# The fourth pair of token tiles of the last stage takes the path of the first three

## The chip, the cores and the metric

The kernel runs on one core of one Trainium2 chip. The core has a matmul engine (TensorE, PE in the profile, with its weight loads shown as PEld), VectorE (DVE), ScalarE (ACT), GpSimd (POOL) and SyncE (SP), each with its own in-order queue of instructions. DMAs are issued here from SP's queue and from ACT's queue. The metric is the device time of one execution in microseconds.

## The reference

Three pieces follow each other: an attention with 32 memory slots, a gated feed-forward layer without an activation, and a second feed-forward layer.

```python
a = softmax(phi, over the sequence)            # batch 4, heads 8, sequence 576, memory 32
k_m, v_m = a.T @ k, a.T @ v                    # per head, 32 x 64
x = softmax(q @ k_m.T / 8) @ v_m               # joined over heads: 2304 tokens x 512
x = ((x @ w_a) * (x @ w_b)) @ w_out            # 512 -> 1536 -> 512
h = x @ w_in                                   # 512 -> 2048
g = h * (1.0 / (1.0 + np.exp(-1.702 * h)))
out = (g @ w_out2).astype(np.float32)          # 2048 -> 512
```

The weights come as 64-bit floats and are decoded on the chip from their two 32-bit words.

## The kernel before

Every product of full precision is made of three matmul passes: each operand is split into a high and a low part (`hi_lo`, lines 305 to 309: ACT copies the high part, DVE or POOL subtracts it from the source for the low one), and high x high, low x high and high x low are added up in PSUM.

The change lies in the last product, g @ w_out2. Its 2304 tokens are nine pairs of tiles (`i` = 0 to 8, 256 tokens each, `NW`), its contraction of 2048 is 16 chunks of 128, and a quarter of it is `K4` = 4 chunks. g lies in DRAM (`g2d`), written by the stage before. For each pair it is loaded transposed (`gated_part`, line 1197), split into high and low parts (`split_part`, line 1220), and multiplied.

- The first `NF` = 3 pairs go by quarters: `load_gated` loads quarter 0 of pairs 0, 1, 2, then quarter 1 of the three, and so on, each 512 KB into a buffer of `f_s`. `proj2` (line 1322) takes the six tiles in that order too, so six PSUM banks are open at a time: each step is 12 matmuls (line 1335) of one tile and one quarter. The first weights chunks of a quarter are needed first, and the decode of the last chunks runs beside the first quarters.
- Pairs 3 and 4 (up to `NS` = 5) go by halves of the contraction: two loads of 1 MB into buffers of `fw_s`; their matmuls are the same `proj2`, one pair at a time.
- Pairs 5 to 8 use seven products in place of eight (`proj2_seven`, line 1349; matmuls in line 1366). Before pair 5 this needs sums of weight blocks, the T weights: `load_pair` (line 1291) loads chunks back from DRAM (`w2d`) by a DMA on ACT's queue (line 1298), DVE and POOL subtract (line 1309), and `hi_lo` splits. Eight such pairs of chunks pass through two buffers, so a batch is two loads, eight subtractions and eight splits, and the next loads wait for the batch before.

The buffers are pieces of the tile `acc`, which the stages before have left. Six quarter buffers exist, F1 to F3 given early, F4 to F6 by `room_last`; a wide buffer is two of them: F5 with F6, F4 with F1, and F2 with F3. In the program as built, the last quarters of pairs 0, 1 and 2 lie in F3, F4 and F5, no quarter uses F6, and the first half of pair 3 goes to F5 with F6. Splits go to six slots in the tiles `attn0` and `attn1` (`attn_92`, `attn_93` in the order's rows); a slot comes free when PE has multiplied the step before in it.

The order of all instructions is made before the launch, by a planner in the kernel (`Order`, lines 95 to 171): streams ask for an engine with an estimated length, or wait for a mark or a buffer, and the planner emits them in the order in which its own clock says they can start. So an instruction that is planned early waits at the head of its engine's in-order queue if what it needs comes later. The weights' raw loads (line 334, `load`) and the decode (`decode_piece`, lines 404 to 453) are streams of the same planner; line 417 is its first step on ACT, line 427 and 432 later ones on DVE, line 448 the high part of a decoded chunk. Outputs are stored by SP (`store`, line 1411), four DMAs for a tile, after ACT or DVE has copied the PSUM bank (`copy`, lines 293 and 295).

The wide buffers are given (`room_last`) when all splits of the first three pairs are planned (the mark "front"), the third of them once the third quarter of pair `NF` is split.

Of the kernel before, what the change touches and what calls it, by code (L numbers as in the profile page):

```python
# [56 lines left out]
def crowded():  # L57
    measured()
    Lengths.pool, Lengths.both, Lengths.slow = 1.3, 1.75, 1.55


def short():
    Lengths.dve, Lengths.act, Lengths.psum = 68, 94, 52
    Lengths.pool, Lengths.both, Lengths.slow = 1.0, 1.0, 1.0
# [110 lines left out]
def tile_mem_attention_moe_moe2(  # L175
# [18 lines left out]
    NT, DM = out.shape  # L194
    F1 = w_o1.shape[0]
    F2 = w_o2.shape[0]
    P = 128
# [19 lines left out]
    K4 = F2 // P // 4  # L217
    NB = 2 * P
# [93 lines left out]
    loaded = {}  # L312
# [415 lines left out]
    def give(slots_, views):  # L728
        slots_.free += [[x, now()] for x in views]
# [202 lines left out]
    win_s, hb_s, f_s, fw_s, sb_s, tb_s = Slots(), Slots(), Slots(), Slots(), Slots(), Slots()  # L932
    wo2_t, blocks = {}, []

    def views(m, n, count, o=0):
        return [m[:, o + i * n:o + (i + 1) * n] for i in range(count)]
# [79 lines left out]
    def room_chunks(*flat):  # L1016
        for x in flat:
            od.mark(now(), "room", "o2", len(wo2))
            wo2.append(x.rearrange("p (i f) -> p i f", i=2))
# [4 lines left out]
    def room_last():  # L1024

        short()
        od.handicap[DVE] = W1
        used = wt["o1", NG1 - 1][0]
        room_chunks(*views(g1_m, CN, 3), *views(used, CN, 2), *views(big["eff_b"], CN, 1))
        for x, o, n in (  # L1030
            (big["y0"], 0, 14), (big["y0"], 18 * DM, 3), (eff_m, 0, 4), (attn_m[0], 4 * SN, 1),
            (attn_m[1], 2 * SN, 5), (big["eff_b"], CN, 2), (p2_rest[0], 0, 4),
        ):
            blocks.extend(x.rearrange("p (i f) -> p i f", i=2) for x in views(x, BN, n, o))
        for q in order:
            for j in range(2):
                for u in range(2):
                    yield "mark", "g2", q, j, u
        n = KD * 2 * N2
        give(f_s, views(acc, FN, 1, n + 2 * FN))  # L1040
        give(tb_s, views(acc, 2 * DM, 2))
        for p in range(F2 // P // 2):
            od.spawn(PT, load_pair(p))
        for c, x in enumerate(views(acc, FN, 2, n), len(pieces) - 3):
            yield "mark", "raw", c
            give(f_s, [x])
        t = yield "mark", "wo2", F2 // P - 1
        crowded()
        od.mark(t, "decoded")
        yield "mark", "front"  # L1050
        wide = views(acc, 2 * FN, 3, n)
        give(fw_s, wide[:2])
        yield "mark", "sb", NF, 2 * K4, 0
        give(fw_s, wide[2:])
        for p in range(F2 // P // 2):
            yield "mark", "wt", p
        short()
        give(dm_s, views(acc, DM, 4))
# [133 lines left out]

    NF, NS, NW = 3, 5, NT // NB

    def gated_part(s, i, o, e):
        t = 0.0
        for g in range(o // G2, (e - 1) // G2 + 1):
            for n in range(i * NB // N2, ((i + 1) * NB - 1) // N2 + 1):  # L1200
                for j in range(2):
                    t = max(t, (yield "mark", "g2", (g, n // 2), j, n % 2))
        f = s[0].rearrange("p (c t) -> p c t", c=e - o)
        nc.sync.dma_start(
            out=f, in_=g2d[o * P:e * P, i * NB:(i + 1) * NB].rearrange("(c p) t -> p c t", p=P)
        )
        od.load(max(t + 2500.0, s[1]), 1.7 * (e - o) * P * NB * 4, "f", i, o)
        loaded["f", i, o] = s, f

    def load_gated():  # L1210
        for o in range(0, 4 * K4, K4):
            for i in range(NF):
                s = yield "slot", f_s
                yield from gated_part(s, i, o, o + K4)
        for i in range(NF, NW):
            for o in (0, 2 * K4):
                s = yield "slot", fw_s
                yield from gated_part(s, i, o, o + 2 * K4)

    def split_part(t, src, *key):  # L1220
        b = yield "slot", sb_s
        loaded[key] = b
        od.spawn(4, split_into(max(t, b[1]), b, src, key))

    def split_into(t, b, src, key):
        t = yield from hi_lo(t, b[0][:, HI], b[0][:, LO], src, K4 * P)
        od.mark(t, *key)

    def split_gated():
        for o in range(0, 4 * K4, K4):  # L1230
            for i in range(NF):
                t = yield "mark", "f", i, o
                slot, f = loaded.pop(("f", i, o))
                for s in range(2):
                    yield from split_part(t, f[:, :, s * P:(s + 1) * P], "sb", i, o, s)
                for s in range(2):
                    t = max(t, (yield "mark", "sb", i, o, s))
                f_s.release(slot, t)
        od.mark(t, "front")
        for i in range(NF, NW):  # L1240
            yield from (split_whole(i) if i < NS else sums_gated(i))

    def split_whole(i):
        for h in (0, 2 * K4):
            t = yield "mark", "f", i, h
            slot, f = loaded.pop(("f", i, h))
            for o in range(0, 2 * K4, K4):
                for s in range(2):
                    yield from split_part(t, f[:, o:o + K4, s * P:(s + 1) * P], "sb", i, h + o, s)
            for o in range(0, 2 * K4, K4):  # L1250
                for s in range(2):
                    t = max(t, (yield "mark", "sb", i, h + o, s))
            fw_s.release(slot, t)
# [9 lines left out]
    def sums_gated(i):  # L1263
        n = K4 * P
        parts = {}
        ts = {}
        for h in (0, 2 * K4):
            ts[h] = yield "mark", "f", i, h
            slot, f = loaded.pop(("f", i, h))
            x = f.rearrange("p (c k) t -> p c k t", k=2)  # L1270
            parts[h] = slot, {
                a: x[:, :, k, s * P:(s + 1) * P]
                for a, k, s in ((A11, 0, 0), (A12, 1, 0), (A21, 0, 1), (A22, 1, 1))
            }
        for name in LAST:
            a = PRODUCTS[name][0]
            for h in (0, 2 * K4):
                t, f = ts[h], parts[h][1]
                if a in MERGE:
                    dst, in0, in1, op, before = MERGE[a]  # L1280
                    for x in before:
                        t = max(t, (yield "mark", "sw", i, h, x))
                    ts[h] = t = yield from combine(t, f[dst], f[in0], f[in1], op, n)
                yield from split_part(t, f[HOME[a]], "sw", i, h, a)
        for h in (0, 2 * K4):
            t = 0.0
            for name in LAST:
                t = max(t, (yield "mark", "sw", i, h, PRODUCTS[name][0]))
            fw_s.release(parts[h][0], t)

    def load_pair(p):

        t = max((yield "mark", "w2d", 2 * p), (yield "mark", "w2d", 2 * p + 1))
        for x in blocks[4 * p:4 * p + 4]:
            wo2_t.setdefault(p, []).append(x)
        m = yield "slot", tb_s
        x = m[0].rearrange("p (k j f) -> p k j f", k=2, j=2)
        nc.scalar.dma_start(
            out=x.rearrange("p k j f -> p k (j f)"),
            in_=w2d[2 * p * P:(2 * p + 2) * P, :].rearrange("(k p) f -> p k f", p=P),  # L1300
        )
        od.load(max(t, m[1]), 2 * P * DM * 4, "pair", p)
        t = max((yield "mark", "pair", p), (yield "mark", "decoded"))
        b11, b12, b21, b22 = (x[:, k, j] for k in range(2) for j in range(2))
        n = DM // 2
        for i, (dst, in0, in1) in enumerate(
            ((b11, b12, b11), (b12, b22, b12), (b22, b22, b11), (b21, b21, b22))
        ):
            t = yield from combine(t, dst, in0, in1, ALU.subtract, n)
            od.spawn(PT, split_t(t, wo2_t[p][i], dst, p, i))  # L1310
        for i in range(4):
            t = max(t, (yield "mark", "wt", p, i))
        tb_s.release(m, t)
        od.mark(t, "wt", p)
# [117 lines left out]
    def main():  # L1432
# [80 lines left out]
        for q in order[1:]:  # L1513
# [3 lines left out]
            if q == (NG2 - 1, 1):  # L1517
                room_split(*views(attn_m[0], SN, 4), *views(attn_m[1], SN, 2))
        od.spawn(9, room_last())
        yield from proj2([(i, s) for i in range(NF) for s in range(2)])  # L1520
        for i in range(NF, NW):
# [66 lines left out]
```

## Time and profile before

| | us |
|---|---|
| median of 3 runs (lowest, highest) | 790.88 (789.92, 791.01) |
| the profiled execution | 790.42 |
| its span on the core | 788.6 |
| PE busy | 772.0 (98%) |
| DVE busy | 638.9 (81%) |
| ACT busy | 417.8 (53%) |
| POOL busy | 365.2 (46%) |

The span is the time from the first to the last instruction of the program on the core; the execution's own time has 1.82 us more. In the page's forty slices PE shows 9 tenths or more in all but the first, the last and one that shows 7, at 651 to 670 us. The last product runs from 584 us to the end.

### The profile page before, as it was taken

How to read it: one execution, taken by the hardware profiler on the slowest of the kernel's cores; microseconds unless marked ns; L12 is line 12 of the kernel's file. 1: busy time of each engine (PE TensorE's matmuls, PEld its weight loads, DVE VectorE, ACT ScalarE, POOL GpSimd, SP SyncE). 2: the span in 40 equal slices, each digit the busy share in tenths (PEclk: the TensorE clock that was granted, in tenths of full speed). 3: DMA queues.
4: the chain of work that ended last, by engine and by line, in shares of the span. 5: the costliest groups of instructions: out<-in, count | busy, mean ns of one | idle time of the engine just before them, and what ended most of it. 6: DMA issues, size and time to landing. Idle time of an engine off the chain costs nothing.

```text
span 788.6 us, 14299 instructions
## 1 busy us (share of the span) xinstructions
PE 772.0 (98%) x5216; PEld 711.6 (90%) x5216; DVE 638.9 (81%) x1135; ACT 417.8 (53%) x925; POOL 365.2 (46%) x343
## 2 busy tenths in 40 slices
PE   8999999999999999999999999999999997999997
PEld 7777789999899899989999999999998885889997
DVE  4888978999999997977989778777867878547886
ACT  4567768564645655445565555555544445434442
POOL 1224225553645644436799655333341046453563
PEclk9999999999999999999999999999999998999999
DMA  8866400122213221230013545455598738624421
GB/s 297 311 190 196 148 25 28 55 81 81 81 54 108 81 81 53 72 90 1 1 65 101 183 159 172 149 164 174 208 309 271 226 135 257 215 75 134 135 81 28
DMA packets 70151, 103.96 MB, mean 132 GB/s; under 512 B 5824, under 2 KB 48832, under 8 KB 70080
## 3 DMA queue, kind: packets, MB, share of 16 engines
q1 hardware_dynamic: 64768, 93.84, 37.3%
q10 hardware_dynamic: 5312, 9.21, 3.3%
q8 instruction: 41, 0.67, 0.4%
q14 instruction: 30, 0.25, 0.1%
HBM read 75.24 MB, written 27.79 MB: 131 GB/s over the span
## 4 chain that ended last, share of the span: by engine, by line
PE 83%; DVE 5%; DMA 4%; ACT 3%; issue 2%; POOL 1%; ACTq 0%; POOLq 0%; DVEq 0%; SPq 0%
PE bank L1135 22%; PE bank L831 18%; PE bank L1366 10%; PE bank L864 10%; PE bank L887 9%; PE bank L1335 6%; PE bank L787 3%; DMA raw<-in_moe_w_out_dram 2%; PE bank L619 1%; PE bank L575 1%; DMA raw<-in_moe_w_b_dram 1%; DVE attn L302 1%; PE bank L756 1%; PE bank L494 1%; DMA acc<-w2d 1%
## 5 line engine op out<-in xcount | busy, mean ns | idle before, releaser
L1177 DVE TENSOR_TENSOR acc<-bank,acc 128x384 f32<-128x384 f32 x168 | 89.7, 553 | 31.8 <-PE bank L1135 20.2
L302 DVE TENSOR_TENSOR attn<-acc,attn 128x512 fp32r<-128x512 f32 (+1 forms) x93 | 88.0, 967 | 30.7 <-ACT attn L308 30.6
L302 POOL TENSOR_TENSOR acc<-acc 128x512 f32<-128x512 f32 (+2 forms) x59 | 76.2, 1306 | 55.7 <-DVE attn L302 30.5
L308 ACT ACTIVATE attn<-acc 128x512 fp32r<-128x512 f32 (+2 forms) x114 | 66.6, 603 | 62.4 <-PE bank L1366 18.7
L1187 ACT ACTIVATE acc<-acc 128x384 f32<-128x384 f32 x96 | 49.3, 523 | 53.1 <-DVE acc L1177 52.2
L844 ACT ACTIVATE gr<-bank 128x288 f32<-128x288 f32 x96 | 38.9, 405 | 64.0 <-PE bank L831 60.9
L302 POOL TENSOR_TENSOR y<-gr,y 128x288 fp32r<-128x288 f32 x40 | 36.3, 908 | 49.9 <-ACT y L308 49.7
L847 DVE TENSOR_TENSOR gr<-bank,gr 128x288 f32<-128x288 f32 x96 | 43.1, 449 | 15.1 <-PE bank L831 8.5
L831 PE MATMUL bank<-attn,eff 128*128 128x288 f32 x384 | 54.4, 296 | 0.0
L831 PEld LDWEIGHTS bank<-attn,eff 128*128 128x128 f32 x384 | 52.1, 188 | 1.3 <-issue 0.9
L864 PE MATMUL bank<-g,whl_b 128*128 128x288 f32 x384 | 52.8, 295 | 0.1
L1135 PE MATMUL bank<-attn,y 128*128 128x384 f32 x288 | 52.3, 335 | 0.0
L864 PEld LDWEIGHTS bank<-g,whl_b 128*128 128x128 f32 x384 | 51.7, 188 | 0.6 <-POOL whl_b L302 0.3
L887 PE MATMUL bank<-y,whl_a 128*128 128x512 f32 (+1 forms) x240 | 51.5, 370 | 0.0
L1335 PE MATMUL bank<-wv,attn 128*128 128x512 f32 x180 | 45.9, 411 | 5.2 <-ACT attn L308 5.2
L1135 PEld LDWEIGHTS bank<-attn,y 128*128 128x128 f32 x288 | 50.1, 188 | 0.0
L419 POOL TENSOR_SCALAR dm<-dm 128x512 f32<-128x512 f32 x21 | 34.7, 1656 | 31.8 <-ACT dm L417 31.7
L887 PEld LDWEIGHTS bank<-y,whl_a 128*128 128x128 f32 x240 | 41.9, 188 | 8.0
L1335 PEld LDWEIGHTS bank<-wv,attn 128*128 128x128 f32 x180 | 35.7, 199 | 13.7 <-ACT attn L308 5.6
L302 POOL TENSOR_TENSOR y<-acc,y 128x256 fp32r<-128x256 f32 (+1 forms) x22 | 19.8, 912 | 59.2 <-ACT y L308 59.2
L302 POOL TENSOR_TENSOR g<-gr,g 128x288 fp32r<-128x288 f32 x28 | 27.0, 966 | 40.8 <-ACT g L308 40.6
L907 DVE TENSOR_TENSOR acc<-bank,acc 128x512 f32<-128x512 f32 (+1 forms) x72 | 38.4, 551 | 5.9 <-PE bank L887 5.2
(269 smaller groups left out, 2022.3 us busy)
## 6 DMA issues: line engine op xcount, KB each, us to landing
g2d<-acc SPq DMA_DIRECT2D x96, 192.0 KB, 2.3
raw<-in_moe_w_out_dram SPq DMA_DIRECT2D x28, 512.0 KB, 4.3
acc<-g2d SPq DMA_DIRECT2D x12, 1024.0 KB, 6.1
raw<-in_moe_w_in_dram SPq DMA_DIRECT2D x16, 512.0 KB, 3.8
acc<-g2d SPq DMA_DIRECT2D x12, 512.0 KB, 5.7
raw<-in_moe_w_a_dram SPq DMA_DIRECT2D x20, 256.0 KB, 2.7
raw<-in_moe_w_b_dram SPq DMA_DIRECT2D x20, 256.0 KB, 3.0
q<-in_q_dram SPq DMA_DIRECT2D x8, 576.0 KB, 6.0
```

What stands on the lines that cost most here:

```text
L302: (nc.gpsimd if e == POOL else nc.vector).tensor_tensor(out=dst, in0=in0, in1=in1, op=op)
L308: nc.scalar.activation(out=hi, in_=src, func=AF.Copy)
L831: nc.tensor.matmul(ps[0][:, :U], e[c][:, sw, i * CW + j * P:i * CW + (j + 1) * P], attn(b, mv, c, u * U, U), start=(n == 0), stop=(n == 3 ...
L844: nc.scalar.activation(out=gr[0], in_=pa_[0][:, :U], func=AF.Copy)
L847: nc.vector.tensor_tensor(out=gr[0], in0=pb[0][:, :U], in1=gr[0], op=ALU.mult)
L864: nc.tensor.matmul(ps[0][:, :U], w[:, sw, j, mb * P:(mb + 1) * P], g1[0][:, j, mv, :], start=(n == 0), stop=(n == 3 * G1 - 1),)
L887: nc.tensor.matmul(ps[0][:, :e - o], w[:, sw, j, mb * P:(mb + 1) * P], g1_all[mv][:, j, o:e], start=(n == 0), stop=(n == 3 * G1 - 1),)
L1135: nc.tensor.matmul(ps[0][:, :N2], w[:, sw, r, :], y[mv][r], start=(n == 0), stop=(n == 5))
L1177: nc.vector.tensor_tensor(out=s[0], in0=ps[0][:, :N2], in1=x[0], op=ALU.add)
L1187: nc.scalar.activation(out=c[0], in_=c[0], func=AF.Gelu_apprx_sigmoid)
L1335: nc.tensor.matmul(ps[i, s][0], b[0][:, sw, c - o, :], wo2[c][:, mv], start=(c == n == 0), stop=(c == 4 * K4 - 1 and n == 2),)
L1366: nc.tensor.matmul(ps[name][0][:, :NB], x[0][:, sw, c, :], moving(b, h // 2 + c, mv), start=(h == c == n == 0), stop=(h > 0 and c == K4 - ...
```

## The change

Two constants stand where one stood: `NQ` = 4 pairs are loaded and split by quarters, while `NF` = 3 pairs are still multiplied together. The four quarters of pair 3 follow the twelve of pairs 0 to 2 in the list `QUARTERS`, which the loading stream and the splitting stream both walk. They take buffers of `f_s`. Pair 3 is multiplied alone, as before. The halves start with pair 4, and the marks "front" and "sb" shift by one pair.

```diff
-        yield "mark", "sb", NF, 2 * K4, 0
+        yield "mark", "sb", NQ, 2 * K4, 0
...
-    NF, NS, NW = 3, 5, NT // NB
+    NF, NQ, NS, NW = 3, 4, 5, NT // NB
...
+    QUARTERS = [(i, o) for o in range(0, 4 * K4, K4) for i in range(NF)]
+    QUARTERS += [(i, o) for i in range(NF, NQ) for o in range(0, 4 * K4, K4)]
+
     def load_gated():
-        for o in range(0, 4 * K4, K4):
-            for i in range(NF):
-                s = yield "slot", f_s
-                yield from gated_part(s, i, o, o + K4)
-        for i in range(NF, NW):
+        for i, o in QUARTERS:
+            s = yield "slot", f_s
+            yield from gated_part(s, i, o, o + K4)
+        for i in range(NQ, NW):
...
     def split_gated():
-        for o in range(0, 4 * K4, K4):
-            for i in range(NF):
-                t = yield "mark", "f", i, o
...
+        for i, o in QUARTERS:
+            t = yield "mark", "f", i, o
...
         od.mark(t, "front")
-        for i in range(NF, NW):
+        for i in range(NQ, NW):
```

In the built program the quarters of pair 3 use F1, F6, F2 and F3. PE's instructions stand in the same order as before. The other queues change near the end of the first three pairs. Behind the splitting stream a line's number is one higher in the changed kernel; the load stays at 1204.

SP's queue, from the last quarter of pair 0 on, in the kernel before (`acc<-g2d` are loads of g, `raw` those of the weights, `out_dram` stores):

```order
L1204 DMA acc<-g2d 128x4x256
L334 DMA raw_80<-in_moe_w_out_dram 128x1024
L1204 DMA acc<-g2d 128x4x256
L334 DMA raw_79<-in_moe_w_out_dram 128x1024
L1204 DMA acc<-g2d 128x4x256
L334 DMA raw_80<-in_moe_w_out_dram 128x1024
L334 DMA raw_79<-in_moe_w_out_dram 128x1024
L1204 DMA acc<-g2d 128x8x256 x2
L1417 DMA out_dram<-dm_84 32x512 x4
```

And in the changed kernel, from the same load on:

```order
L1204 DMA acc<-g2d 128x4x256
L334 DMA raw_80<-in_moe_w_out_dram 128x1024
L1204 DMA acc<-g2d 128x4x256
L334 DMA raw_79<-in_moe_w_out_dram 128x1024
L1204 DMA acc<-g2d 128x4x256 x2
L334 DMA raw_80<-in_moe_w_out_dram 128x1024
L1204 DMA acc<-g2d 128x4x256
L334 DMA raw_79<-in_moe_w_out_dram 128x1024
L1204 DMA acc<-g2d 128x4x256 x2
L1418 DMA out_dram<-dm_84 32x512 x4
```

Two quarter loads of pair 3 stand ahead of the last two raw loads, one before each, and two behind them; the two wide loads are gone from here. The loads of pair 4 stand further on, behind six groups of four stores, where the stores of the sixth tile stood behind two of them.

ACT's queue, from the second batch of T weights on, in the kernel before (`acc<-w2d` are that batch's loads, `y` the high parts of T weights, `attn` the splits of g, lines 293 the copies of PSUM banks):

```order
L1298 DMA acc<-w2d 128x2x512 x2
L293 ACTIVATE dm_84<-bank_76 128x512
L293 ACTIVATE dm_85<-bank_73 128x512
L308 ACTIVATE y_1431<-acc 128x256 x5
L293 ACTIVATE dm_83<-bank_72 128x512
L308 ACTIVATE y_1431<-acc 128x256 x2
L1298 DMA acc<-w2d 128x2x512
L308 ACTIVATE y_1431<-acc 128x256
L293 ACTIVATE acc<-bank_78 128x512
L1298 DMA acc<-w2d 128x2x512
L308 ACTIVATE attn_92<-acc 128x512 x4
```

And in the changed kernel, from the same load on:

```order
L1299 DMA acc<-w2d 128x2x512
L308 ACTIVATE y_1431<-acc 128x256
L293 ACTIVATE dm_84<-bank_76 128x512
L1299 DMA acc<-w2d 128x2x512
L308 ACTIVATE attn_92<-acc 128x512
L293 ACTIVATE dm_85<-bank_73 128x512
L308 ACTIVATE attn_92<-acc 128x512
L308 ACTIVATE y_1431<-acc 128x256
L293 ACTIVATE dm_83<-bank_72 128x512
L308 ACTIVATE attn_92<-acc 128x512
L308 ACTIVATE y_1431<-acc 128x256 x4
L308 ACTIVATE attn_92<-acc 128x512
```

The splits of pair 3 stand inside the second batch, the first right behind its loads, where they stood behind the loads of the third batch. The copy of bank 78 has moved to DVE.

## Rows read from the trace of the kernel before

**Rows 1.** The page's first line.

```profile
span 788.6 us, 14299 instructions
```

**Rows 2.** Waits of PE, whole span: who waited for whom, us, times, longest.

```profile
PE bank L1335 <- ACT attn L308: 5.2, 1, 5.2
```

**Rows 3.** Stretches: length, busy PE PEld DVE ACT POOL, clock, DMA share, GB/s.

```profile
620.00:640.00 20.00, 20.00 (x89) 16.23 (x88) 16.52 (x28) 10.95 (x23) 4.51 (x5) 1.00 0.38 117
...
651.00:656.20 5.20, 0.05 (x2) 0.04 (x1) 3.36 (x6) 2.43 (x6) 2.23 (x3) 0.91 0.83 267
...
658.00:660.00 2.00, 2.00 (x6) 1.58 (x5) 2.00 (x3) 1.98 (x5) 1.38 (x2) 0.50 0.65 202
```

**Rows 4.** Timeline of PE: start, length, line, operation, count, idle before.

```profile
650.15 0.86 PE L1335 MATMUL bank<-eff_b,attn 128*128 128x512 f32 x3
656.16 9.87 PE L1335 MATMUL bank<-wv,attn 128*128 128x512 f32 x30 [5.15 <-ACT attn L308]
665.87 0.40 PE L1335 MATMUL bank<-whl_a,attn 128*128 128x512 f32 x1
...
681.14 7.16 PE L1335 MATMUL bank<-wv,attn 128*128 128x512 f32 x30
688.14 1.56 PE L1335 MATMUL bank<-whl_a,attn 128*128 128x512 f32 x6
...
703.40 1.58 PE L1366 MATMUL bank<-y,attn 128*128 128x256 f32 x12
```

**Rows 5.** Timeline of ACT around the wait.

```profile
642.69 0.90 ACTq L1298 DMA_DIRECT2D acc<-w2d  x2
...
655.07 0.37 ACTq L1298 DMA_DIRECT2D acc<-w2d  x1
655.48 2.19 ACT L308 ACTIVATE attn<-acc 128x512 fp32r<-128x512 f32 x4 [0.49 <-DVE y L302]
```

**Rows 6.** Timeline of SP's queue.

```profile
619.83 5.26 SPq L334 DMA_DIRECT2D raw<-in_moe_w_out_dram  x2
643.24 1.04 SPq L1204 DMA_DIRECT2D acc<-g2d  x2
...
664.45 9.32 SPq L1417 DMA_DIRECT2D out_dram<-dm  x4
```

**Rows 7.** Timeline of DVE: two splits of g.

```profile
618.47 0.69 DVE L302 TENSOR_TENSOR attn<-acc,attn 128x512 fp32r<-128x512 f32 x1
...
642.53 0.68 DVE L302 TENSOR_TENSOR attn<-acc,attn 128x512 fp32r<-128x512 f32 x1
```

**Rows 8.** DMA issues of 619:630, 573:600, 640:645, 656:664: KB each, us to landing.

```profile
raw<-in_moe_w_out_dram SPq DMA_DIRECT2D x2, 512.0 KB, 4.3
...
raw<-in_moe_w_out_dram SPq DMA_DIRECT2D x4, 512.0 KB, 5.6
...
acc<-g2d SPq DMA_DIRECT2D x2, 1024.0 KB, 8.7
...
acc<-g2d SPq DMA_DIRECT2D x2, 1024.0 KB, 6.6
```

**Rows 9.** Timeline, all engines: the last weights chunk.

```profile
633.80 0.69 DVE L302 TENSOR_TENSOR eff_b<-acc,eff_b 128x512 fp32r<-128x512 f32 x1 [0.70 <-ACT eff_b L448]
...
636.23 0.85 PE L1335 MATMUL bank<-eff_b,attn 128*128 128x512 f32 x3
```

**Rows 10.** Timelines of ACT, DVE and POOL: fifth pair's first split, last T weight.

```profile
669.15 0.37 ACTq L1298 DMA_DIRECT2D acc<-w2d  x1
...
669.49 0.69 DVE L302 TENSOR_TENSOR attn<-acc,attn 128x512 fp32r<-128x512 f32 x1 [0.41 <-ACT attn L308]
...
684.24 0.92 POOL L302 TENSOR_TENSOR rest<-acc,rest 128x256 fp32r<-128x256 f32 x1
```

**Rows 11.** The chain that ended last.

```profile
643.11 5.08 DMA acc<-w2d
```

**Rows 12.** Waits of SP's queue, 540 to 789.

```profile
SPq L1417 <- DMA acc<-w2d: 9.4, 3, 6.6
```

More of the change, by code (lines that the diff above doesn't have):

```diff
@@ L1229, in split_gated @@
     def split_gated():
-        for o in range(0, 4 * K4, K4):
-            for i in range(NF):
-                t = yield "mark", "f", i, o
[L1233 to L1238, printed above, removed]
+        for i, o in QUARTERS:
+            t = yield "mark", "f", i, o
+            slot, f = loaded.pop(("f", i, o))
+            for s in range(2):
+                yield from split_part(t, f[:, :, s * P:(s + 1) * P], "sb", i, o, s)
+            for s in range(2):
+                t = max(t, (yield "mark", "sb", i, o, s))
+            f_s.release(slot, t)
         od.mark(t, "front")
-        for i in range(NF, NW):
+        for i in range(NQ, NW):
             yield from (split_whole(i) if i < NS else sums_gated(i))
```

## The prediction

> **What bounds the kernel now.** I read the views from the whole to the place. The page gives a span of 788.6 us [rows 1]; the profiled execution took 790.42 us, so 1.82 us lie around the span. The view of waits, cut to TensorE (PE) over the whole span, has one wait in the last stage: line 1335 waited once, 5.2 us, on ScalarE's (ACT's) line 308 [rows 2]. So there PE sets the time, and every other engine matters only where PE waits.
>
> The PE timeline puts the wait at the start of the fourth token pair: the last matmuls of the first three pairs end at 650.15 + 0.86 = 651.01, the next starts at 656.16 [rows 4]. The table of stretches shows what came with it: PE is busy 0.05 of 5.2 us, the granted clock is 0.91 over that stretch, then 0.50 at 658 to 660, the lower of the two levels, 1.2 GHz in place of 2.4 [rows 3]. The cost of the low clock is read by comparing like with like: the same 30 matmuls (512 columns, moving operand wv) open the fourth pair and the fifth. They take 665.87 - 656.16 = 9.71 us in the fourth and 688.14 - 681.14 = 7.00 us in the fifth [rows 4].
>
> Why did the fourth pair come late? Two causes lie on top of each other. First, its load: issued at 643.24 [rows 6], since its wide buffer covers the quarter buffer F5, which VectorE (DVE) was reading until 642.53 + 0.68 = 643.21 [rows 7]; such a pair of 1 MB loads landed after 8.7 us [rows 8], so near 652. Second, ACT's order: the four first splits of that pair stand behind two loads of the T weights (line 1298), the second issued at 655.07, only when a whole batch of T work was done, and start at 655.48 [rows 5]. A split takes 2.19 / 4 = 0.55 us on ACT [rows 5] and 0.69 us on DVE [rows 7], so the load alone would have held PE until 651.9 + 1.24 = 653.2; the order in ACT's queue did the rest. Both have to go.
>
> **The change, part by part.** *Four quarter loads for two half loads.* Two more loads are issued, 0.5 us each on SP (1.04 us for two [rows 6]), off the path. By the built order they use buffers F1, F6, F2, F3. F1 is free when DVE's split that starts at 618.47 ends, 619.16 [rows 7]; F6 was used by no quarter; F2 and F3 are read a few splits later. So I put the first load at 619.2, right before the raw load of 619.83 [rows 6], the second behind that, near 620.2, the third behind the last raw load, near 619.83 + 5.26 = 625.1, the fourth by 632. A 512 KB load in company took a median of 5.6 us [rows 8]. The data are there by about 638, 13 us before PE wants them at 651.0.
>
> *The splits move ahead of the T batch.* In the new ACT order (second place shown) the fourth pair's first split follows the batch's loads at once, where before a batch stood in between. These loads went out at 642.69 [rows 5] and the order of what leads to them is almost the same, so the first split starts near 645 (their issue of 0.90 us, one copy and a short activation later) and is done by 647: 4 us early. Later tiles of the pair are wanted each 22.26 / 8 = 2.78 us (a pair runs 681.14 to 703.40 [rows 4]) and their splits are mixed into the batch, which lasts until about 657; the eighth is wanted at 651.0 + 7 x 2.78 = 670.5. I cost this at nothing.
>
> *What goes.* The stall, 5.15 us, and the low clock behind it, 9.71 - 7.00 = 2.71 us: 7.86 us.
>
> *SP's queue: the last two raw loads now stand behind two quarter loads.* These raw loads feed the last output weights. The very last is done at 633.80 + 0.69 = 634.49; PE uses it at 636.23 [rows 9], a slack of 1.74 us. The new order of DVE has one 0.69 us operation less between its decode steps (the other weight's low part is moved ahead), so some 2.4 us. A raw load took 4.3 us there and 5.6 us in the crowded stretch 573 to 600 [rows 8]. Bounds: 0 to 1.3 us per raw load, 2.6 us if both delays add. I take one, 1.3 us, since the DMA engines were busy only 0.38 of 620 to 640 [rows 3]: hidden. If the cover went, 2.6 - 2.4 = 0.2 us.
>
> Here a page speaks against the change. The rows have 5.6 us for a 512 KB load in company and 6.6 us for a 1 MB one [rows 8]: half the size saves little. The Trainium skill, DMA: Bandwidth & Descriptors, section Bandwidth, goes further and makes it a rule: batch transfers to 1 MiB or more, since smaller ones reach a lower share of the peak. By the rows as I use them, with loads that overlap, the sum stays at 7.86; by the rule taken to the end, loads in series, it is rival C.
>
> *What is late next: the fifth pair.* PE gets to it at 651.0 + 22.26 = 673.3 instead of 681.14, while the T work keeps its own pace. Its first split stands on ACT right behind the next two T loads; before, the second of those went out at 669.15, and DVE ended that split at 669.49 + 0.69 = 670.18 [rows 10]. What does the change do to that time? The batch without splits in it took 655.07 - 643.11 = 12.0 us, the one with eight splits 669.15 - 655.07 = 14.1 us [rows 5, 10, 11]: 2.1 us for eight. The change spreads the same eight, and moves one PSUM copy from ACT to DVE. So the two batches together stay at 26.1 us: about 670.5, 2.8 us before PE. Bounds: 0.8 us earlier, since the first batch's weights landed in 5.08 us beside two 1 MB loads [rows 11] and a raw load of the same size nearly alone in 4.3 [rows 8], or 8 x 0.69 = 5.5 us later if every split fell on the batches' chain. I take 0, nearest to the measured batches: nothing lost. The pair's load, too, now stands behind all 24 stores of the first three pairs, where before four of them stood behind it. It has until 673.3 - 6.6 - 1.24 = 665.5. The last stores follow a copy on ACT behind the batch's second T load, near 643.11 + 12.0 + 1.3 (five of the eight splits) = 656.4; stores did wait for such loads to land, three times, 9.4 us in all [rows 12], so I add one landing of 5.08 and 2 for the copy and the issues: 663.5, in time by 2.0 us.
>
> *The T weights themselves* must be whole when the sixth pair begins, now 695.5; before the last piece was done at 684.24 + 0.92 = 685.16 [rows 10]: 10 us of cover. From there on each pair is PE-bound with loads tied to PE's own progress, and shifts as a whole.
>
> **Sum.** 790.42 - 7.86 = 782.56 us for the profiled execution; it lies 0.46 us under the median of 790.88, so 783.0 us for a median.
>
> **Rivals.**
> A, the forecast: 782.0 to 784.3.
> B, a new wait takes the old one's place at the fifth pair. For it: only 2.8 us of margin on ACT's queue and 2.0 on its load, both downstream of a T batch that now has splits inside it. Against it: the same amount of work as before, and less DMA traffic beside it. At the bound, 5.5 us late, PE waits 2.7 us; with a low-clock cost in the old proportion (2.71 per 5.15 us) another 1.4 us, so 783.0 + 4.1 = 787.1; for 1 us, 784.5. Middle 785.5.
> C, the raw loads suffer: quarter loads in series ahead of the last raw load delay it by a whole 5.6 us, PE waits 5.6 - 2.4 = 3.2 us at 636 and pays 1.7 us for the clock: 787.9. For it the crowded 5.6 us; against it, the engines are busy well under half of the time in that stretch.
> D, the change does not do what it says: the load was hidden and ACT's order alone bounds, or the other way round, and the stall stays: 790.9. The built order speaks against it, since both move.
> E, slower: the fifth pair's load waits in SP's queue behind the 24 stores. From an issue at 665.5 on PE loses each microsecond; from 665.5 + 5.15 = 670.6 on, with its own low clock, the kernel is slower than before: 791 to 795, say 793. For it: one group of four stores there took 9.32 us before [rows 6]. Against it: that group followed two 1 MB loads, which are now behind the stores.
>
> **How the numbers follow.** A 0.72, B 0.16, C 0.04, D 0.03, E 0.05. Differences under 0.2% (1.6 us) count as no change for this kernel. Faster: A, B, C, 0.92; same: D, 0.03; slower: E, 0.05. The time is A's, 783.0. The range takes A below, less a run's scatter of about 1 us, and B above to its bound: 781.9 to 787.1; left out are C, D, E and the edges, some 0.15.
>
> **What would show it.** Right: no wait of line 1336 on line 308 near 651, 30 opening matmuls of the fourth pair in 7.0 us, a granted clock of 1.00 from 640 to 680, quarter loads issued near 619, 620, 625 and 630, PE at the sixth pair near 695.5. Wrong: a PE wait at 636 (C), at 673 (B, E), or a clock under 1 anywhere after 640.

## The result, and the profile after

The kernel with the change took 782.58 us (median of four runs, 782.24 to 782.93), the kernel before, run beside it, 790.87 us (four runs, 789.92 to 791.01): a ratio of 0.9898 [0.9881, 0.9915], 8.3 us less. The forecast was 783.0 us. The profiled execution took 782.89 us, 7.53 less than the profiled one of before.

The page's first line, for [rows 1]:

```profile
span 781.0 us, 14294 instructions
```

The view of PE's waits, for [rows 2], has no entry left between 560 and 785 us; what stands there over the whole span is short and lies in the first stages:

```profile
PE bank L555 <- ACT et L547: 1.4, 1, 1.4
```

PE's timeline, for [rows 4]:

```profile
636.49 1.13 PE L1336 MATMUL bank<-eff_b,attn 128*128 128x512 f32 x3
...
650.69 0.86 PE L1336 MATMUL bank<-eff_b,attn 128*128 128x512 f32 x3
651.39 7.16 PE L1336 MATMUL bank<-wv,attn 128*128 128x512 f32 x30
658.39 1.56 PE L1336 MATMUL bank<-whl_a,attn 128*128 128x512 f32 x6
...
673.65 7.16 PE L1336 MATMUL bank<-wv,attn 128*128 128x512 f32 x30
...
695.91 1.34 PE L1367 MATMUL bank<-y,attn 128*128 128x256 f32 x10
```

The fourth pair starts at 651.39 with no idle time before it, and its first 30 matmuls take 658.39 - 651.39 = 7.00 us. The fifth pair starts 681.14 - 673.65 = 7.49 us earlier than before, which is nearly all of the 7.53.

The table of stretches, for [rows 3]:

```profile
620.00:640.00 20.00, 20.00 (x87) 15.94 (x86) 15.58 (x27) 9.82 (x19) 2.29 (x3) 1.00 0.69 231
651.00:656.20 5.20, 5.20 (x24) 4.22 (x23) 4.72 (x7) 3.33 (x8) 4.21 (x5) 1.00 0.41 108
658.00:660.00 2.00, 2.00 (x10) 1.62 (x9) 0.38 (x1) 0.09 (x1) 1.67 (x2) 1.00 0.78 243
```

PE fills the 5.2 us that it stood still, and the granted clock is 1.00 where it was 0.91 and 0.50. The load has moved: the DMA engines are busy 0.69 of 620 to 640 (0.38 before).

SP's queue, for [rows 6]:

```profile
615.91 4.21 SPq L1204 DMA_DIRECT2D acc<-g2d  x2
620.35 0.34 SPq L334 DMA_DIRECT2D raw<-in_moe_w_out_dram  x1
620.75 0.42 SPq L1204 DMA_DIRECT2D acc<-g2d  x1
624.90 0.35 SPq L334 DMA_DIRECT2D raw<-in_moe_w_out_dram  x1
625.46 6.80 SPq L1204 DMA_DIRECT2D acc<-g2d  x2
```

The second load of the first row and the three behind it are the fourth pair's quarters, between the raw loads.

ACT, for [rows 5], then the fifth pair's first split on DVE, for [rows 10]:

```profile
645.40 0.42 ACTq L1299 DMA_DIRECT2D acc<-w2d  x1
645.86 0.63 ACT L308 ACTIVATE attn<-acc 128x512 fp32r<-128x512 f32 x1 [0.51 <-issue]
...
669.98 0.89 ACTq L1299 DMA_DIRECT2D acc<-w2d  x2
...
671.64 0.69 DVE L302 TENSOR_TENSOR attn<-acc,attn 128x512 fp32r<-128x512 f32 x1 [1.35 <-ACT attn L308]
```

The fourth pair's first split starts on ACT at 645.86, not 655.48, and the fifth pair's is done at 671.64 + 0.69 = 672.33, 1.3 us before PE.

The DMA view of 617 to 632 us, for [rows 8]; its four loads of g are the fourth pair's quarters:

```profile
acc<-g2d SPq DMA_DIRECT2D x4, 512.0 KB, 7.1
raw<-in_moe_w_out_dram SPq DMA_DIRECT2D x2, 512.0 KB, 7.1
```

And the view of the weight loads' waits (PEld) of 560 to 785:

```profile
PEld bank L1336 <- DVE eff_b L302: 0.4, 1, 0.4
```

A raw load took 7.1 us in place of 4.3, and the last weights chunk came a little late: its three matmuls took 1.13 us, 0.28 more than the 0.85 of [rows 9]. DVE's last operation on that chunk started 636.14 - 633.80 = 2.34 us later than in [rows 9]:

```profile
636.14 0.69 DVE L302 TENSOR_TENSOR eff_b<-acc,eff_b 128x512 fp32r<-128x512 f32 x1 [0.70 <-ACT eff_b L448]
```

### The profile page after: what moved, and what is told of

Its sections match the earlier page's. It is cut to its first block, busy times and chain, and to the rows that moved or that the text cites. A ratio compares the mean times of both kernels' runs of the same rounds, so it can differ in the third digit from the quotient of the medians.

```text
span 781.0 us, 14294 instructions
## 1 busy us (share of the span) xinstructions
PE 768.4 (98%) x5216; PEld 708.6 (91%) x5216; DVE 638.9 (82%) x1132; ACT 416.9 (53%) x924; POOL 367.8 (47%) x347
## 4 chain that ended last, share of the span: by engine, by line
PE 92%; DVE 3%; ACT 2%; DMA 1%; issue 1%; POOL 1%; ACTq 0%; DVEq 0%; POOLq 0%; SPq 0%
PE bank L1135 22%; PE bank L831 18%; PE bank L1336 14%; PE bank L1367 10%; PE bank L864 10%; PE bank L887 10%; PE bank L787 3%; PE bank L619 1%; PE bank L575 1%; DMA kv<-in_v_dram 1%; PE bank L756 1%; PE bank L494 1%; ACT et L547 0%; DMA phi<-in_phi_dram 0%; DVE mx L541 0%
## 5 line engine op out<-in xcount | busy, mean ns | idle before, releaser
L1177 DVE TENSOR_TENSOR acc<-bank,acc 128x384 f32<-128x384 f32 x168 | 89.7, 553 | 31.8 <-PE bank L1135 21.2
L302 DVE TENSOR_TENSOR attn<-acc,attn 128x512 fp32r<-128x512 f32 (+2 forms) x94 | 91.3, 994 | 25.6 <-ACT attn L308 25.5
L302 POOL TENSOR_TENSOR acc<-acc 128x512 f32<-128x512 f32 (+2 forms) x63 | 80.0, 1283 | 46.9 <-DVE attn L302 23.2
L1336 PE MATMUL bank<-wv,attn 128*128 128x512 f32 x180 | 43.2, 394 | 0.0
L417 ACT ACTIVATE dm<-raw 128x512 f32<-128x512 f32 x41 | 26.9, 666 | 28.7 <-DMA raw<-in_moe_w_b_dram 12.1
```

The lines of the kernel that those rows point to most:

```text
L302: (nc.gpsimd if e == POOL else nc.vector).tensor_tensor(out=dst, in0=in0, in1=in1, op=op)
L1177: nc.vector.tensor_tensor(out=s[0], in0=ps[0][:, :N2], in1=x[0], op=ALU.add)
L1336: nc.tensor.matmul(ps[i, s][0], b[0][:, sw, c - o, :], wo2[c][:, mv], start=(c == n == 0), stop=(c == 4 * K4 - 1 and n == 2),)
```

## The experiments

Eight runs, in two groups of four, each group on a chip of its own. The kernel before ran beside both groups: a median of 788.95 us (23 runs, 786.73 to 790.79) beside the first and 789.09 us (17 runs, 787.39 to 791.62) beside the second. So it varies by 4 us. The changed kernel, run again beside the second group, took 782.24 us: there the gain, by the medians, is 6.85 us and not 8.3.

**Load early, order late.** The changed kernel with the fourth pair's splits planned behind the T batch, its quarter loads as early as they are.

```diff
         for i, o in QUARTERS:
+            if (i, o) == (NF, 0):
+                yield "mark", "wt", 2
+                yield "mark", "wt", 3
             t = yield "mark", "f", i, o
```

> The changed kernel with its four quarter loads of pair 3 as they are, but the splits of that pair planned only after the second batch of T weights is split, so that they stand on ACT behind the third batch's loads, as before. Theory (either of load and order is enough to hold PE, so both had to go): the data lie there by 640, yet PE waits at about 651.4 for ACT until near 657, some 5 us, pays 2.7 us for the low clock, and the time is 790 to 791.5. Rival (the load alone held PE): no wait, 782.6.

Measured: 789.37 us (787.13 to 792.45), ratio to before 1.0009 [0.9995, 1.0022]. The whole gain is gone. The rival, no wait, is out. The stall is the theory's; the time lies 0.6 us under its range, which went with a kernel before of 790.9, where that kernel took 788.95 here. PE's wait in the last stage, and its timeline:

```profile
PE bank L1339 <- ACT attn L308: 4.6, 1, 4.6
```

```profile
655.72 8.92 PE L1339 MATMUL bank<-wv,attn 128*128 128x512 f32 x30 [4.63 <-ACT attn L308]
664.48 1.55 PE L1339 MATMUL bank<-whl_a,attn 128*128 128x512 f32 x6
```

Early data alone gain nothing that shows. The run fits the theory, that either of the two holds PE, and it fits the order alone holding it; the next run tells these apart.

**Order early, load late.** The kernel before with its two 1 MB loads, but the planner counts the fourth pair as loaded at once, so that its splits stand in ACT's queue ahead of the T batch. What really arrives is waited for as ever.

```diff
         od.load(max(t + 2500.0, s[1]), 1.7 * (e - o) * P * NB * 4, "f", i, o)
+        if i == NF:
+            od.mark(s[1], "f", i, o)
         loaded["f", i, o] = s, f
```

> The kernel before with its two 1 MB loads of pair 3 as they are, issued near 643, but the splits planned as if these had landed at once, so that they stand on ACT right behind the second batch's T loads, as in the changed kernel. Theory (either is enough): PE now waits for the landing, near 652, and a split, until 653.2: 2.2 us in place of 5.15, with a low clock in proportion (1.2 us) 786.4, without it 785.2. ACT stands blocked meanwhile, so the T batch ends some us later and the fifth pair may wait too, up to 2 us. Rival (order alone held PE): 783. Rival (the load alone): 790.9.

Measured: 783.01 us (782.2 to 783.09), ratio 0.9921 [0.9908, 0.9935]. The theory fell, the rival holds. SP's and ACT's timelines, and PE's:

```profile
642.12 1.05 SPq L1204 DMA_DIRECT2D acc<-g2d  x2
...
649.63 0.63 ACT L308 ACTIVATE attn<-acc 128x512 fp32r<-128x512 f32 x1 [6.46 <-DMA acc<-g2d]
...
650.41 7.33 PE L1337 MATMUL bank<-wv,attn 128*128 128x512 f32 x30
```

ACT's split stands at the head of its queue for 6.46 us until the load lands, and still the pair is ready when PE is: PE has no wait in the last stage, only weight loads that wait 0.6 us. The first half landed at about 649.6, 7.5 us after its issue at 642.12. The trace is of the fastest of the five runs; three of the others took 783.0 to 783.1, and no trace shows what they waited for.

**Clock kept up.** The kernel before with 20 matmuls of no use ahead of the fourth pair's first.

```diff
+                if (i, s, o) == (NF, 0, 0):
+                    for _ in range(20):
+                        nc.tensor.matmul(ps[i, s][0], wo2[0][:, HI, :P], wo2[0][:, HI], start=True, stop=True)
```

> The kernel before with 20 extra matmuls of 512 columns, on operands that are long there, into the PSUM bank that the fourth pair is about to start, ahead of its first matmul; they take 20 x 0.233 = 4.7 us of the 5.15 us wait. Theory (the low clock follows PE's idleness and costs 2.71 us): granted clock 1.00 throughout, the fourth pair's first 30 matmuls in 7.0 us, time 788.2. Rival (the slow start of the pair has another cause, its fresh operands or the traffic beside it): 9.7 us for the 30 matmuls and 790.9.

Measured: 787.93 us, ratio 0.9986 [0.9975, 0.9998], so 0.2 to 2.0 us less than before, against 2.7 expected. PE's and ACT's timelines:

```profile
650.93 4.72 PE L1335 MATMUL bank<-wv 128*128 128x512 f32 x20
657.14 7.41 PE L1338 MATMUL bank<-wv,attn 128*128 128x512 f32 x30 [1.49 <-ACT attn L308]
664.38 1.53 PE L1338 MATMUL bank<-whl_a,attn 128*128 128x512 f32 x6
```

```profile
656.04 0.37 ACTq L1298 DMA_DIRECT2D acc<-w2d  x1
```

The clock held, 1.00 from 656 to 664: the 30 matmuls took 664.38 - 657.14 = 7.24 us, not 9.71. (The 0.24 us over 7.00 are not clock; a weight load waited 0.4 us there for DVE's split.) In this execution the second T load went out at 656.04, 0.97 us later than in [rows 5], yet the 30 matmuls ended 665.87 - 664.38 = 1.49 us earlier: 2.46 us for the clock at an equal T batch. That the median gained less is explained, though not shown, by the next run: where the T batch is early the 20 matmuls, which end near 655.6, hold PE themselves.

**The kernel before once more.**

> The kernel before, unchanged, with a profile of its own, to see where its scatter of some 4 us from run to run comes from. Theory: PE's wait before the fourth pair ends with the T batch on ACT, whose time differs from run to run; the time then goes with that wait, about 1.5 us for each us of it (wait and low clock, 7.86 us for 5.15), and everything up to PE's arrival near 651 agrees within 1 us. Rival: the scatter arises elsewhere, and the wait stays at 5.2 us in a run of another time.

Measured: 789.4 us (787.18 to 791.33), ratio 0.9999 [0.9986, 1.0012]; the profiled execution took 787.18 us, 3.24 less than the one of before. SP's, ACT's and PE's timelines of it:

```profile
617.58 5.32 SPq L334 DMA_DIRECT2D raw<-in_moe_w_out_dram  x2
640.89 1.05 SPq L1204 DMA_DIRECT2D acc<-g2d  x2
...
640.35 0.90 ACTq L1298 DMA_DIRECT2D acc<-w2d  x2
...
652.71 0.37 ACTq L1298 DMA_DIRECT2D acc<-w2d  x1
653.12 2.19 ACT L308 ACTIVATE attn<-acc 128x512 fp32r<-128x512 f32 x4 [0.49 <-DVE y L302]
...
653.80 9.01 PE L1335 MATMUL bank<-wv,attn 128*128 128x512 f32 x30 [2.77 <-ACT attn L308]
662.65 1.55 PE L1335 MATMUL bank<-whl_a,attn 128*128 128x512 f32 x6
```

Against [rows 4 to 6], the raw loads go out 619.83 - 617.58 = 2.25 us earlier, the T loads 2.34 and 2.36, and PE's stall is 5.15 - 2.77 = 2.38 us shorter; the 30 matmuls take 8.85 us, 0.86 less. 2.38 + 0.86 = 3.24, the whole difference, and PE arrives at the stall at the same time, 651.03 (651.01 before). So between these two executions the difference is there at the raw loads already and is carried through the T batch into the stall. The run with the 20 matmuls, whose queues are those of before, fits: DVE's last operation on the last weights chunk started at 634.69 there, at 633.80 before and at 631.48 in the repeat, and the second T load followed at 656.04, 655.07 and 652.71, 21.2 to 21.4 us behind each time. That all of the scatter is this, and what shifts the raw loads, is not shown. It is 1.36 us of time for each us of stall here, not 1.5.

**The changed kernel once more.**

> The changed kernel once more, beside the experiments, for its scatter. Theory: with no wait left before the fourth pair, the scatter of the kernel before is gone with it: all runs within 1 us, 782 to 783, and a weight load of PE that waits 0.2 to 0.5 us for the last output weight near 636. Rival: the scatter stays, since it comes from an earlier stage: runs 3 us apart.

Measured: 782.24 us (782.04 to 782.74), ratio 0.9909 [0.9892, 0.9926]. The scatter is 0.7 us in five runs, where the kernel before beside it had 4.2 in 17 and 4.2 in 12. The weight load at 636 did not wait this time; the DMA view has

```profile
raw<-in_moe_w_out_dram SPq DMA_DIRECT2D x2, 512.0 KB, 5.2
```

**Raw loads first.** The changed kernel, the fourth pair's quarter loads held back behind the last raw load.

```diff
         for i, o in QUARTERS:
+            if (i, o) == (NF, 0):
+                yield "mark", "raw", len(pieces) - 1
             s = yield "slot", f_s
```

> The changed kernel with the four quarter loads of pair 3 issued only behind the last raw load. Theory (the two quarter loads slow the last two raw loads from 4.3 to 7.1 us, which makes the last weights chunk 0.3 us late for PE): raw landings back at 4.3 to 5.6 us, no wait of PE's weight load on the last chunk, quarters there by 640, no stall at pair 3, 782.0 to 782.6, the same within what can be told. Rival (the lateness comes from the new DVE order alone): the raw loads still take 7 us or the wait stays. Rival on the other side (the four loads come too late and the stall returns in part): 784 or more.

Measured: 782.21 us (781.88 to 782.61), ratio 0.9915 [0.9902, 0.9928]. No weight load waits in the last stage, and the raw loads are back at their old time beside loads that now come after them:

```profile
acc<-g2d SPq DMA_DIRECT2D x4, 512.0 KB, 6.1
raw<-in_moe_w_out_dram SPq DMA_DIRECT2D x2, 512.0 KB, 4.5
```

The intervals overlap with the changed kernel's own repeat, and the medians are 0.03 us apart: no gain that shows.

**Five pairs by quarters**, without and with the raw loads first. (The mark before the last wide buffers goes too, since it would wait for a pair that is no longer loaded there.)

```diff
-    NF, NQ, NS, NW = 3, 4, 5, NT // NB
+    NF, NQ, NS, NW = 3, 5, 5, NT // NB
```

> The fifth pair too is loaded and split by quarters of the contraction; the rest as in the changed kernel. Theory: the change paid only because PE stood still at the fourth pair; it arrives at the fifth with 1.3 us to spare, so 782 to 783.2, as the changed kernel. Rival 1: quarters are better in themselves, 781.5 or less. Rival 2: quarter loads ahead of the raw loads and splits inside the T batches cost PE waits: 784 or more.

> Fifth pair by quarters as well, and the fourth pair's quarter loads held back behind the last raw load. Theory: 782.0 to 782.6, as with the raw loads first alone (782.2): PE has no wait left in the last stage, so nothing can be gained there. Rival: another 0.5 us or more below that, if the fifth pair still costs something; or 784 and more, if eight quarters stand in the way of the T weights.

Measured: 783.28 us, ratio 0.9922 [0.9907, 0.9938], and 783.34 us, 0.9919 [0.9904, 0.9935]: 1.0 and 1.1 us above the changed kernel beside them, a little over what the theory allowed (783.2 and 782.6). Neither is a gain. The first lies above every run of the changed kernel there (783.07 to 784.0 against 782.04 to 782.74); the second overlaps with it. In the first, PE is at the sixth pair as early as in the changed kernel, 695.09 against 695.15. What is lost comes later; the chain that ended last has two loads of g in it:

```profile
730.95 5.16 DMA acc<-g2d
...
751.57 5.24 DMA acc<-g2d
```

They went out at 730.95 and 751.57, 2.8 us later than the same loads of the changed kernel (728.16 and 748.77), and PE and its weight loads wait on DVE's split of them:

```profile
PE bank L1366 <- DVE attn L302: 0.4, 2, 0.2
...
PEld bank L1366 <- DVE attn L302: 1.1, 3, 0.4
```

At these three waits, and nowhere else, PE falls behind the changed kernel: it is 0.06 us ahead at the sixth pair, 0.19 behind after the first wait, 0.83 after the second and 1.53 after the third, and its last three matmuls start at 776.31 against 774.80. Of the 1.96 us between the two profiled executions (784.0 and 782.04) the span has 1.3; the rest lies around the span (2.4 us against 1.74) and is not explained. So the later pairs were tied to PE with little to spare, and quarters of a fifth pair push their loads back. Which buffer or queue does it stays open.

## Why the prediction was right, and what in it was not

**The sum.** The stall and the low clock were put at 5.15 + 2.71 = 7.86 us. Both went: no idle time at 651, 7.00 us for the 30 matmuls. The 0.37 us by which the fifth pair gained less (7.49) is PE's later arrival. The last three matmuls before the fourth pair start at 650.69, 0.54 us after those of [rows 4] (650.15). Of this, 0.28 is the late weights chunk at 636. The other 0.26 is there when the last product begins, so it comes from a stage that the change leaves alone; before and after:

```profile
584.42 18.02 PE L1335 MATMUL bank<-wv,attn 128*128 128x512 f32 x78
...
584.68 18.02 PE L1336 MATMUL bank<-wv,attn 128*128 128x512 f32 x78
```

Against it stand 0.16 us: the stall was counted from the end that the profile gives a matmul (650.15 + 0.86), and the next one of an unbroken row starts 0.16 us before such an end (651.39 against 650.69 + 0.86 = 651.55). The time does not hang on the execution that the sum was read from: the repeat of before, 3.24 us faster, gives 787.18 - 2.77 - 1.85 = 782.56 too. The predicted signs hold: no wait near 651, a clock of 1.00 from 640 to PE's last matmul, quarter loads near 619.7, 620.8 and up to 632, PE at the sixth pair at 695.91 (said: 695.5). Of the signs of being wrong only a trace of C's came, the weight load that waited 0.4 us at 636.

**"Two causes lie on top of each other ... Both have to go": this step failed.** ACT's order alone held PE. With the order mended and the load left late, 783.01; with the load mended and the order left late, 789.37. The step made the load's part too large in two terms. It took 8.7 us from issue to landing, but that median is of both halves, and the first split needs only the first. The DMA view of the kernel before, cut to 643 to 643.5 us, has that load alone:

```profile
acc<-g2d SPq DMA_DIRECT2D x1, 1024.0 KB, 7.5
```

And it added both splits, 1.24 us, where PE began 0.68 us after ACT did (656.16 against 655.48 [rows 4, 5]): the first two of the three passes use g's high part alone. From the issue at 643.24 [rows 6] this gives 643.24 + 7.5 + 0.68 = 651.4, not 653.2. So the load alone would have cost PE some 0.4 us in that execution, and none in the repeat of before, where it was issued at 640.89; both are estimates from these rows. The forecast was not hurt, and its number could not show the error, since the change mends both. But of the change's two parts the moved splits earn nearly all. What the early quarters add is not shown: 783.01 us without them against 782.21 for the kernel with the raw loads first, on the same chip, with ranges that overlap.

**The raw loads**, one term put at nothing: right in the sum, mis-sized in its bound. 4.3 to 5.6 us were the bounds for a load; 7.1 was measured in one execution, 5.2 in another, 4.5 with the raws first. At 7.1 the slack of 2.4 us was used up and 0.28 us were lost; at 5.2 nothing was. Rival C's 3.2 us did not come. Nor did the rule behind it, in the Trainium skill, DMA: Bandwidth & Descriptors, section Bandwidth (transfers of 1 MiB or more), decide here: the kernel with halves and the order mended (783.01 us) was not faster than those with quarters (782.24 and, on the same chip, 782.21).

**The fifth pair.** Said: about 670.5, 2.8 us before PE; measured: 672.33 and 1.3 us. The late weights chunk is in this too: the T loads behind it went out later, the second one at 645.40 where the step took 643.11. In the changed kernel's repeat, where the raw loads landed after 5.2 us, that load went out at 642.81, and the fifth pair's first split was done at 668.22 + 0.69 = 668.91, 4.0 us before PE (672.89). So the margin differs by 2.7 us between two executions. The bound of 5.5 us later was not approached, and rival B did not come, though its margin was as thin as it said. The pair's load was issued at 663.68 (said: 663.5), so E did not come. D's outcome, a stall that stays, did not come either; the first of its two readings, that the load was hidden and ACT's order alone bounds, was nearly right, but the change moves the order too.

**The clock in rival B** ("in the old proportion", 2.71 per 5.15): no proportion holds. Stalls of 5.15, 4.63 and 2.77 us cost 2.71, 1.76 and 1.85 us more in the 30 matmuls (9.71, 8.76 and 8.85 against 7.00). The tables of stretches, of the kernel before, of load early with order late, and of the repeat of before, then of the clock kept up:

```profile
656.00:664.00 8.00, 7.84 (x22) 6.23 (x23) 7.51 (x9) 5.96 (x15) 5.97 (x6) 0.62 0.68 210
...
656.20:664.00 7.80, 7.80 (x28) 6.10 (x27) 7.14 (x9) 5.35 (x12) 5.97 (x5) 0.78 0.73 221
...
654.00:660.00 6.00, 6.00 (x19) 4.44 (x19) 5.65 (x8) 4.24 (x10) 4.33 (x4) 0.72 0.68 213
...
656.00:664.00 8.00, 6.86 (x29) 5.36 (x30) 6.54 (x9) 5.76 (x13) 5.02 (x5) 1.00 0.73 223
```

With the two levels 0.50 and 1.00, a mean of 0.62 over 8 us is 0.38 x 8 / 0.5 = 6.1 us at the lower one; the next two rows give 3.4 us each, though the stalls were 4.63 and 2.77 us, and the last none, after 1.49 us of idleness behind the 20 matmuls.

**The size.** 783.0 was said for a median and 782.58 found. The other two groups show that the gain itself is not one number: the profiled execution of before lay at the slow end of its scatter (790.42 of 786.7 to 791.6), and against 789.09 the change gains 6.85 us.

## What to carry to other kernels

When an instruction that the bounding engine waits for sits behind others in an in-order queue, ask first what stands ahead of it there: here the early load was worth nothing until the order moved, and the order alone was worth nearly all. For the landing time that matters, take the first transfer of a group and not the group's median. And look at the scatter: here the bounding engine waited on a side chain, the difference between two executions was that chain's, and the scatter went with the wait.

## What the runs showed of the hardware

The last two 512 KB raw loads landed after a median of 4.3 us (the kernel before) and 4.5 us (raw loads first) with no quarter load between them, and after 7.1 and 5.2 us with quarter loads between (two executions of the changed kernel). Of the two 1 MB loads issued together the first landed after 7.5 us, though the median of the pair is 8.7. What a stall costs in clock is not in proportion to it: the granted clock stood at 0.50 for 3.4 us after a stall of 4.63 us and for 3.4 us after one of 2.77 us, and the same 30 matmuls took 1.76 and 1.85 us longer.
